# The first batch item in another order: score tile 4 and the second half of q behind score tile 0, fewer zero matmuls, value and score products ahead of hidden tile 1

## The chip, the core and the metric

The kernel runs on one core of one Trainium2 chip. A core has a matrix engine (TensorE, in the profile PE, with its weight loads as PEld), a vector engine (VectorE, DVE), a scalar engine (ScalarE, ACT), a general engine (GpSimd, POOL) and a queue engine (SyncE, SP), each with its own instruction stream. They wait for each other through semaphores. Matrix products land in an accumulator memory that TensorE writes and that VectorE or ScalarE must empty. The metric is device microseconds of one launch, the median of several runs.

## The reference

Four batch items of attention feed a two-branch feed-forward block. What is computed, cut to what matters:

```python
# q, k, v: [4, 8, 768, 64]; sort_net: [4, 8, 8, 8]
P = sort_net
for _ in range(5):                       # Sinkhorn: rows, then columns
    P = exp(P - max(P)); P /= sum(P, -1) + 1e-9; P /= sum(P, -2) + 1e-9
k_sorted = einsum('bhij,bhjcd->bhicd', P, k_blocks)      # 8 blocks of 96 tokens
v_sorted = einsum('bhij,bhjcd->bhicd', P, v_blocks)
attn = softmax(q_block @ k_sorted_block.T / 8)           # block against its own block
x = (attn @ v_sorted_block).transpose(0, 2, 1, 3).reshape(3072, 512)
out = maximum(x @ w1, x @ w2) @ w_out                    # 512 -> 1024 -> 512
```

The kernel uses max(h1, h2) = relu(h1 - h2) + h2: it multiplies x by w1 - w2, takes relu, multiplies by w_out, and adds x times the product w2 @ w_out, which it computes once.

## The kernel before

**Work and names.** Each of the four batch items passes through the same steps. `sort_k` (three calls) and `sort_v` (four calls for one item) mix the blocks of k and v by the Sinkhorn matrix. `q_transposes(b, half)` turns q, in two halves: half 0 has head pairs 0 and 1, half 1 has head pairs 2 and 3. `scores(b, u)` makes score tile u of eight (SC[u] below): u = 4 x ih + hp, block half ih and head pair hp, so tiles 0, 1, 4 and 5 read half 0 of q and tiles 2, 3, 6 and 7 read half 1. Its eight products (L461) land in an accumulator, and ScalarE writes their exponentials into a tile e (L469). `values(b, u)` (VA[u]) multiplies e by v with a column of ones (L488); VectorE takes the reciprocal of the sums (L499) and writes the normalised x (L505). `x_transposes(b, t)` turns two neighbouring value tiles into xT: t = 0 needs value tiles 0 and 1, t = 1 needs 2 and 3, t = 2 needs 4 and 5, t = 3 needs 6 and 7; for item 0 TensorE turns them (L526) and ScalarE copies them out (L108). `moe_h(b, ch, t)` makes hidden tile t of token half ch: eight products (L590) and relu into g. For item 0, hidden tile 0 is made in two parts: the products on head pairs 0 and 2 once xT 0 is there, those on 1 and 3 once xT 1 is there. `w_difference(t)` subtracts a quarter of w2 from w1 (L194): quarters 0 and 1 on GpSimd, 2 and 3 on VectorE; hidden tile t needs quarter t. `w2_transposes(t, eng)` turns half of w2 (L551), and `w_product` multiplies it by w_out (L570). `moe_out` makes output tiles (L617).

**Zero matmuls.** `keep_streaming(ps, n, by, most)` issues products of a tile of zeros into an accumulator, n columns in all, `most` columns at a time; nothing reads them. The kernel begins with 88 of 138 columns (L666), and has 6 of 512 in each of the last two Sinkhorn rounds; the calls with a third number above 0 in the list below have them too. `q_transposes` for item 0 begins each half with one transposition of zeros (L362).

**What sets the order.** Every engine executes its instructions in the order in which the Python program issues them. For item 0 this order is written out by hand, from L665 to L722. Three engines take part in it: TensorE makes the products, VectorE and ScalarE empty the accumulators as the letters "D" and "A" say. There are four accumulators of 4 KB per partition, all of one pool, so a new product has to wait until one of them has been read. After item 0 a planner interleaves hidden and output tiles of one item (the `units`) with the attention steps of the next: after unit n it first issues the list `tail[n]`, then so many steps that they keep pace with the units' cost. `evac` without a letter and `moe_h` take the engine that has less load by the planner's own count. GpSimd issues the loads from HBM; SyncE issues the stores of the output and, from item 1 on, the transposing DMAs.

Of the kernel before, what the change touches and what calls it, by code (L numbers as in the profile page):

```python
# [16 lines left out]
def kernel(  # L17
# [21 lines left out]
    B, H, S, D = q.shape  # L39
# [26 lines left out]
    def ps_f32(name):  # L66
        return psum.tile([128, 1024], FP32, tag="ps", name=name)

    def ps_bf16(name):
        return psum.tile([128, 2048], BF16, tag="ps", name=name)  # L70
# [6 lines left out]
    def keep_streaming(ps, n, by=None, most=512):  # L77

        w0 = fill[:, 0:128] if by is None else late[by]
        while n > 0:  # L80
            w = min(n, most)
            nc.tensor.matmul(ps[:, 0:w], w0, fill[:, 0:w], start=True, stop=True)  # L82
            n -= w
# [265 lines left out]
    def q_transposes(b, half, eng=None):  # L349

        if half == 0:
            qT[b] = qpool.tile([128, HP, R, 128], BF16, tag="qT", name="qT")
        if b > 1:
            hps = slice(half * 2, half * 2 + 2)
            nc.sync.dma_start_transpose(
                out=qT[b][:, hps].rearrange("p h r c -> p (h r) c"),
                in_=q_pair[b][:, hps].rearrange("p h r d -> p (h r d)"),
            )
            return
        ps = ps_bf16("tq_ps")  # L360
        if b == 0:
            nc.tensor.matmul(  # L362
                ps[:, 0:128], fill[:, 0:128], ident, is_transpose=True, start=True, stop=True
            )
        for n in range(2 * R):
            hp, r = half * 2 + n // R, n % R
            c = slice(n * 128, (n + 1) * 128)
            for h2 in range(2):
                nc.tensor.matmul(  # L369
                    ps[h2 * 64 : h2 * 64 + 64, c],  # L370
                    q_raw[b][:, hp + 4 * h2, r * D : (r + 1) * D],
                    ident,
                    is_transpose=True,
                    start=True,
                    stop=True,
                )
        evac(
            qT[b][:, half * 2 : half * 2 + 2].rearrange("p h r c -> p (h r c)"),
            ps[:, 0 : 2 * R * 128],
            2 * R * 128,  # L380
            two_x=True,
            eng=eng,
        )

    def sort_k(b, t, n=0, eng=None):
        kv = k_raw[b].rearrange("p (c d) -> p c d", d=D)
        ps = ps_f32("k_ps")
        keep_streaming(ps, n)

        for c in range(16):  # L390
            for par in range(2):
                m = (c + 8 * par) % 16
                r0 = par * 64
                nc.tensor.matmul(  # L394
                    ps[r0 : r0 + 64, m * 64 : (m + 1) * 64],
                    kv[r0 : r0 + 64, t * 16 + m, :],
                    bd_k[b][r0 : r0 + 64, :],
                    start=True,
                    stop=True,
                )  # L400
        evac(
            kT[b][:, 0 : 32 * BLK]
            .rearrange("p (m ch c) -> p ch m c", ch=2, m=32)[:, :, :, t * 16 : (t + 1) * 16],
            ps.rearrange("p (c ch m) -> p ch m c", ch=2, m=32),
            1024,
            eng=eng,
        )
# [44 lines left out]
    def scores(b, u, n=0):  # L452
        ih, hp = divmod(u, HP)
        ps = ps_f32("s_ps")
        keep_streaming(ps, n)
        for ii in range(4):
            i = ih * 4 + ii
            for h2 in range(2):
                rows = slice(h2 * 64, h2 * 64 + 64)
                rhs = qT[b][rows, hp, :, i * PB : (i + 1) * PB]  # L460
                nc.tensor.matmul(  # L461
                    ps[:, h2 * 512 + ii * 128 : h2 * 512 + ii * 128 + BLK],
                    kT[b][rows, (hp * 8 + i) * BLK : (hp * 8 + i) * BLK + 128],
                    rhs,
                    start=True,
                    stop=True,
                )
        e = e_bufs[(b * 8 + u) % NE]
        nc.scalar.activation(  # L469
            out=e[:, 0 : 8 * BLK].rearrange("p (t c r) -> p t c r", t=8, r=R),  # L470
            in_=ps[0:BLK]
            .rearrange("p (t f) -> p t f", t=8)[:, :, 0:BLK]
            .rearrange("p t (r c) -> p t c r", r=R),
            func=AF.Exp,
            scale=scale,
        )
        load["A"] += 800
        e_tiles[b, u] = e

    def values(b, u, n=0):  # L480
        ih, hp = divmod(u, HP)
        e = e_tiles.pop((b, u))
        m0 = (b % 2) * 64
        ps = ps_f32("o_ps")
        keep_streaming(ps, n)
        for h2 in range(2):
            for ii in range(4):
                nc.tensor.matmul(  # L488
                    ps[:, h2 * 512 + ii * 65 : h2 * 512 + (ii + 1) * 65],
                    e[:, (h2 * 4 + ii) * BLK : (h2 * 4 + ii) * BLK + 128],  # L490
                    v_sb[:, m0 + (hp + 4 * h2) * 8 + ih * 4 + ii, 0:65],
                    start=True,
                    stop=True,
                )
        ov = ps[0:BLK].rearrange("p (t f) -> p t f", t=2)[:, :, 0 : 4 * 65].rearrange(
            "p t (i f) -> p t i f", f=65
        )
        rs = xpool.tile([BLK, 2, 4], FP32, tag="rs", name="rs")
        nc.vector.reciprocal(out=rs, in_=ov[:, :, :, 64])  # L499
        if hp % 2 == 0:  # L500
            x_tiles[b, ih, hp // 2] = xpool.tile(
                [BLK, 2, 4, 2, D], BF16, tag="x", name="x", bufs=4
            )
        x = x_tiles[b, ih, hp // 2][:, :, :, hp % 2, :]
        nc.vector.tensor_tensor(  # L505
            out=x,
            in0=ov[:, :, :, 0:D],
            in1=rs.to_broadcast([BLK, 2, 4, D]),
            op=ALU.mult,
        )  # L510
        load["D"] += 900
# [35 lines left out]
    def w2_transposes(t, eng):  # L547
        ps = ps_bf16("tw_ps")
        for n in range(16):
            fb, dmt = t * 4 + n // 4, n % 4  # L550
            nc.tensor.matmul(  # L551
                ps[:, n * 128 : (n + 1) * 128],
                w2_sb[:, dmt, fb * 128 : (fb + 1) * 128],
                ident,
                is_transpose=True,
                start=True,
                stop=True,
            )
        return lambda: evac(
            w2T[:, t * 4 : t * 4 + 4, :].rearrange("p f d -> p (f d)"),  # L560
            ps,
            2048,
            two_x=True,
            eng=eng,
        )
# [32 lines left out]
    def moe_h(b, ch, t, eng=None, hps=(0, 2, 1, 3), n=0):  # L598
        moe_h_products(b, ch, t, hps, n)
        ps = h_ps[t]  # L600
        g = gpool.tile([128, 2, TCH], BF16, tag="g", name="g")
        src = ps.rearrange("p (t f) -> p t f", t=2)[:, :, 0:TCH]
        if (eng or pick((200 + 2 * TCH) / 1.2, (130 + 2 * TCH) / 0.96)) == "A":
            nc.scalar.activation(out=g, in_=src, func=AF.Relu)  # L604
        else:
            nc.vector.tensor_scalar(
                out=g, in0=src, scalar1=0.0, scalar2=None, op0=ALU.max
            )
        g_tiles[b, ch, t] = g
# [53 lines left out]
        return SC, VA, TR  # L663

    first, second, both = slice(0, 64), slice(64, 128), slice(0, 128)  # L665
    keep_streaming(ps_f32("fill_ps"), 88 * 138, most=138)  # L666
    for it in range(5):
        sinkhorn(it)
        if it < 2:
# [9 lines left out]
    turn_v(first, "D", 80, 96)  # L679

    SC, VA, TR = att(0)
    sort_k(0, 0, 2048, "A")
    sort_k(0, 1, 0, "D")
    sort_k(0, 2, 0, "A")
    sort_v(0, 0, 0, "D")
# [2 lines left out]
    sort_v(0, 2, 0, "A")  # L688
    sort_v(0, 3, 0, "D")
    SC[0]()  # L690
    SC[1]()
    q_transposes(0, 1, "D")
    SC[4]()
    VA[0]()
    scores(0, 2, 1024)
    VA[1]()
    SC[3]()
    values(0, 2, 1024)
    x_transposes(0, 0, "A")
    values(0, 3, 512)  # L700
    SC[5]()
    moe_h_products(0, 0, 0, (0, 2), 512)
    x_transposes(0, 1, "A")
    VA[4]()
    SC[6]()
    moe_h(0, 0, 0, "A", (1, 3))
    SC[7]()
    VA[5]()
    moe_h(0, 0, 1, "A")
    x_transposes(0, 2, "A")  # L710
    VA[6]()
    w_difference(2)
    VA[7]()
    w2_transposes(0, "D")()
    w_difference(3)
    for b in range(1, B):
        selections(b)
    for c, n, m in [(2, 1, 0), (3, 3, 1)]:
# [5 lines left out]
    def turn(rows, c0):  # L724
        turn_v(rows, "D", c0, c0 + 24)
        load["D"] += 850

    def load_rest():
# [1 line left out]
        load_k(2)  # L730

    tail = {
        2: [TR[3], lambda: w2_transposes(1, "A")(), load_rest],
        4: [lambda: turn(second, 0)],
        5: [lambda: block_diagonals([(0, 2), (1, 1), (1, 2), (1, 3)], 2)],
        6: [lambda: turn(second, 24), lambda: turn(second, 48)],
# [6 lines left out]
    for b in range(B):  # L743
# [21 lines left out]
        if b < B - 1:  # L765
            qs = [lambda half=half: q_transposes(b + 1, half) for half in range(2)]
            ks = [lambda t=t, b=b: sort_k(b + 1, t) for t in range(3)]
            SC, VA, TR = att(b + 1)
# [65 lines left out]
```

## Time and profile before

| what | value |
|---|---|
| median of 5 runs | 170.29 us (169.89 to 170.39) |
| the profiled execution | 170.39 us, of which 168.4 us are the span from the first to the last instruction |
| TensorE, matmuls | 162.7 us busy, 97% of the span |
| ScalarE, VectorE, GpSimd | 85.7 us, 75.8 us, 28.6 us |
| 11.7 to 17.5 us (sorting of k and v, half 0 of q) | TensorE busy 5.78 of 5.80 us |
| 17.5 to 24 us (scores, value products) | TensorE busy 6.41 of 6.50 us |
| 24 to 33 us (hidden tiles 0 to 2, the rest of the value products) | TensorE busy 8.31 of 9.00 us |
| 33 to 62 us | TensorE busy 29.00 of 29.00 us |

The page is one profiled execution. A busy time is the union of an engine's instructions; a matmul counts as busy from its start to its modelled end, about 0.2 us for a small one, while the next one starts 15 to 60 ns after it. So an engine that is busy all the time has not necessarily done as much as it could, and zero matmuls count as busy as well. The wait before an instruction is given as idle time, with the instruction that ended it.

### The profile page before, as it was taken

What the parts mean: (1) busy time and instruction counts of PE and PEld (TensorE: products, weight loads), DVE (VectorE), ACT (ScalarE), POOL (GpSimd) and SP (SyncE); (2) the same over time, 40 slices, a digit from 0 to 9 for tenths busy, and PEclk for the clock granted to TensorE, in tenths of its full rate; (3) what the DMA queues carried; (4) which work ended last, traced back from release to release, by engine and by line L of the source; (5) the groups of instructions that cost most, each with busy time, mean ns of one, the idle gap of its engine ahead of it and who ended that gap; (6) DMA issues with size and microseconds to landing.
All of it is one profiled execution on the core that took longest, in us unless ns stands there. A gap on an engine that the chain in (4) does not pass through costs nothing.

```text
span 168.4 us, 4544 instructions
## 1 busy us (share of the span) xinstructions
PE 162.7 (97%) x2018; PEld 97.8 (58%) x2018; DVE 75.8 (45%) x174; ACT 85.7 (51%) x104; POOL 28.6 (17%) x44
## 2 busy tenths in 40 slices
PE   7999999999999999999999999999999999999991
PEld 7949766755765454566654545557545456654451
DVE  4978874948454359437734434205443160000011
ACT  3587878474674353176774504457605406642020
POOL 7866585232302003000000000000000000000000
PEclk9999999999999999999999999999999999999999
DMA  3999999999999994999700344690054255000333
GB/s 46 205 204 198 199 208 206 222 202 204 218 212 206 205 238 81 181 150 234 163 0 4 88 130 141 99 292 5 0 36 139 57 167 171 0 0 0 125 143 110
DMA packets 30243, 23.11 MB, mean 137 GB/s; under 512 B 16720, under 2 KB 25168, under 8 KB 30224
## 3 DMA queue, kind: packets, MB, share of 16 engines
q0 software_dynamic: 10880, 12.59, 44.8%
q1 hardware_dynamic: 19200, 10.17, 25.5%
q8 instruction: 16, 0.26, 0.7%
q10 hardware_dynamic: 144, 0.07, 0.1%
q14 instruction: 3, 0.02, 0.0%
HBM read 25.17 MB, written 6.29 MB: 187 GB/s over the span
## 4 chain that ended last, share of the span: by engine, by line
PE 93%; DVE 2%; ACT 1%; issue 1%
PE out_ps L617 36%; PE h_ps L590 25%; PE fill_ps L82 6%; PE o_ps L488 4%; PE wc_ps L570 4%; PE k_ps L394 4%; PE s_ps L461 4%; PE v_ps L415 2%; PE tq_ps L369 2%; PE v_ps L436 1%; PE tx_ps L526 1%; ACT v_sb L108 1%; PE k_ps L82 1%; DVE q_pair L343 1%; PE tw_ps L551 1%
## 5 line engine op out<-in xcount | busy, mean ns | idle before, releaser
L617 PE MATMUL out_ps<-wo_sb,g 128*128 128x512 bf16 (+2 forms) x200 | 48.5, 371 | 0.3 <-DVE x L505 0.3
L590 PE MATMUL h_ps<-xT,w_sb 128*128 128x384 bf16 x256 | 44.7, 326 | 0.6 <-ACT xT L108 0.4
L590 PEld LDWEIGHTS <-w_sb 128*128 128x128 bf16 x256 | 24.0, 98 | 16.4 <-DVE w_sb L194 0.4
L108 ACT COPY o<-out_ps 128x1024 f32<-128x1024 f32 x11 | 11.1, 1012 | 40.4 <-issue 22.8
L604 ACT ACTIVATE g<-h_ps 128x768 bf16<-128x768 f32 x27 | 21.9, 811 | 16.4 <-PE h_ps L590 16.4
L469 ACT ACTIVATE e<-s_ps 96x768 bf16<-96x768 f32 x32 | 24.3, 805 | 6.1 <-PE s_ps L461 6.1
L617 PEld LDWEIGHTS <-g 128*128 128x128 bf16 x200 | 16.9, 98 | 15.7 <-DVE x L505 0.4
L617 PE MATMUL out_ps<-wc,xT 128*128 128x512 bf16 (+2 forms) x100 | 24.8, 370 | 0.0
L505 DVE TENSOR_TENSOR x<-o_ps,rs 96x512 bf16<-96x512 f32 x32 | 22.0, 687 | 1.1
L499 DVE RECIPROCAL rs<-o_ps 96x8 f32<-96x8 f32 x32 | 6.5, 203 | 33.8 <-PE o_ps L488 33.6
L617 PEld LDWEIGHTS <-xT 128*128 128x128 bf16 x100 | 9.6, 97 | 11.2
L488 PEld LDWEIGHTS <-e 96*128 96x128 bf16 x256 | 11.7, 98 | 6.0 <-ACT e L469 0.2
L488 PE MATMUL o_ps<-v_sb,e 96*128 96x65 bf16 x256 | 12.9, 193 | 0.0
L652 DVE COPY o<-out_ps 128x512 f32<-128x512 f32 (+1 forms) x2 | 1.2, 624 | 25.0 <-PE out_ps L617 25.0
L110 DVE CAST kT<-k_ps 128x1024 bf16<-128x1024 f32 x5 | 6.0, 1222 | 12.3 <-PE k_ps L394 12.3
L110 DVE CAST v_sb<-v_ps 96x1024 bf16<-96x1024 f32 x8 | 9.6, 1215 | 2.5 <-PE v_ps L415 1.7
L108 ACT CAST v_sb<-v_ps 96x1024 bf16<-96x1024 f32 x8 | 8.0, 1005 | 3.3 <-PE v_ps L415 1.9
L136 POOL DMA_DIRECT2D q_raw<-in_q_dram x7 | 6.4, 934 | 19.3 <-DVE rs L499 14.0
L461 PEld LDWEIGHTS <-kT 64*128 64x128 bf16 x256 | 6.1, 94 | 6.1 <-issue 5.2
L82 PEld LDWEIGHTS <-fill 128*128 128x128 bf16 x98 | 8.4, 121 | 1.6 <-DVE fill L73 1.2
L82 PE MATMUL fill_ps<-fill 128*128 128x138 bf16 x88 | 7.8, 272 | 1.2 <-DVE fill L73 1.2
L461 PE MATMUL s_ps<-qT,kT 64*128 64x96 bf16 x256 | 8.8, 204 | 0.1
(77 smaller groups left out, 137.8 us busy)
## 6 DMA issues: line engine op xcount, KB each, us to landing
out_dram<-o SPq DMA_DIRECT2D x11, 512.0 KB, 3.0
k_raw<-in_k_dram POOLq DMA_DIRECT2D x12, 256.0 KB, 12.4
v_raw<-in_v_dram POOLq DMA_DIRECT2D x6, 384.0 KB, 12.8
q_raw<-in_q_dram POOLq DMA_DIRECT2D x3, 768.0 KB, 11.6
w_sb<-in_moe_w_dram POOLq DMA_DIRECT2D x4, 256.0 KB, 9.5
w_sb<-in_moe_w_dram POOLq DMA_DIRECT2D x2, 512.0 KB, 11.3
wo_sb<-in_moe_w_out_dram POOLq DMA_DIRECT2D x2, 512.0 KB, 14.8
v_raw<-in_v_dram POOLq DMA_DIRECT2D x3, 256.0 KB, 4.8
```

The source lines that it names most:

```text
L82: nc.tensor.matmul(ps[:, 0:w], w0, fill[:, 0:w], start=True, stop=True)
L108: nc.scalar.copy(out=out_ap, in_=in_ap)
L110: nc.vector.tensor_copy(out=out_ap, in_=in_ap)
L394: nc.tensor.matmul(ps[r0 : r0 + 64, m * 64 : (m + 1) * 64], kv[r0 : r0 + 64, t * 16 + m, :], bd_k[b][r0 : r0 + 64, :], start=True, stop=True,)
L461: nc.tensor.matmul(ps[:, h2 * 512 + ii * 128 : h2 * 512 + ii * 128 + BLK], kT[b][rows, (hp * 8 + i) * BLK : (hp * 8 + i) * BLK + 128], rhs ...
L469: nc.scalar.activation(out=e[:, 0 : 8 * BLK].rearrange("p (t c r) -> p t c r", t=8, r=R), in_=ps[0:BLK] .rearrange("p (t f) -> p t f", t=8 ...
L488: nc.tensor.matmul(ps[:, h2 * 512 + ii * 65 : h2 * 512 + (ii + 1) * 65], e[:, (h2 * 4 + ii) * BLK : (h2 * 4 + ii) * BLK + 128], v_sb[:, m0 ...
L505: nc.vector.tensor_tensor(out=x, in0=ov[:, :, :, 0:D], in1=rs.to_broadcast([BLK, 2, 4, D]), op=ALU.mult,)
L570: nc.tensor.matmul(ps[:, 0:512], w2T[:, fb, dmt * 128 : (dmt + 1) * 128], wo_sb[:, fb, :], start=(fb == 0), stop=(fb == NFB - 1),)
L590: nc.tensor.matmul(h_ps[t][:, m * 512 : m * 512 + TCH], w1_sb[:, hp, fb * 128 : (fb + 1) * 128], xT[:, b % 2, ch, hp % 2, hp // 2, :], sta ...
L604: nc.scalar.activation(out=g, in_=src, func=AF.Relu)
L617: nc.tensor.matmul(dst, g_tiles[b, ch, m // 2][:, m % 2, off : off + 128] if m < NFB else xT[:, b % 2, ch, hp % 2, hp // 2, off : off + 12 ...
```

## The change

It concerns item 0 alone, and the zeros.

1. The zero stream at the start has 86 products of 142 columns where it had 88 of 138.
2. The first `sort_k` begins with 1024 zero columns (two products) where it had 2048 (four).
3. The zero transposition stays ahead of half 0 of q, and is gone ahead of half 1.
4. Score tile 4 follows score tile 0, then half 1 of q, then score tile 1. Before, the order was 0, 1, half 1, 4.
5. Score tile 2 has no zeros ahead of it (it had two products); value tile 1 has one (it had none), value tile 2 one (it had two), value tile 3 none (it had one).
6. Value tile 4 follows value tile 3, ahead of score tile 5. Before, it stood behind x transposition 1. Score tile 6 and value tile 5 follow x transposition 1; score tile 7 and value tile 6 stand ahead of hidden tile 1. Before, value tile 5 stood ahead of it and value tile 6 behind x transposition 2.
7. VectorE's subtraction of quarter 3 stands ahead of its copy of the first turned half of w2.
8. The second half of w2 is turned, and the next q and k are loaded, after unit 3 where they were after unit 2.

```diff
         ps = ps_bf16("tq_ps")
-        if b == 0:
+        if b == 0 and half == 0:
             nc.tensor.matmul(
...
-    keep_streaming(ps_f32("fill_ps"), 88 * 138, most=138)
+    keep_streaming(ps_f32("fill_ps"), 86 * 142, most=142)
...
-    sort_k(0, 0, 2048, "A")
+    sort_k(0, 0, 1024, "A")
...
     SC[0]()
+    SC[4]()
+    q_transposes(0, 1, "D")
     SC[1]()
-    q_transposes(0, 1, "D")
-    SC[4]()
     VA[0]()
-    scores(0, 2, 1024)
-    VA[1]()
+    SC[2]()
+    values(0, 1, 512)
     SC[3]()
-    values(0, 2, 1024)
+    values(0, 2, 512)
     x_transposes(0, 0, "A")
-    values(0, 3, 512)
+    VA[3]()
+    VA[4]()
     SC[5]()
     moe_h_products(0, 0, 0, (0, 2), 512)
     x_transposes(0, 1, "A")
-    VA[4]()
     SC[6]()
+    VA[5]()
     moe_h(0, 0, 0, "A", (1, 3))
     SC[7]()
-    VA[5]()
+    VA[6]()
     moe_h(0, 0, 1, "A")
     x_transposes(0, 2, "A")
-    VA[6]()
     w_difference(2)
     VA[7]()
-    w2_transposes(0, "D")()
+    w2T_ready = w2_transposes(0, "D")
     w_difference(3)
+    w2T_ready()
...
     tail = {
-        2: [TR[3], lambda: w2_transposes(1, "A")(), load_rest],
+        2: [TR[3]],
+        3: [lambda: w2_transposes(1, "A")(), load_rest],
```

## The prediction

> **What bounds the kernel now.** I read the page first, then the chain of work that ended last, then the timeline of the first item instruction by instruction. The page's chain says that TensorE's own stream sets the time:
>
> ```profile
> PE 93%; DVE 2%; ACT 1%; issue 1%
> ```
>
> So a change pays only where it takes TensorE work out, or a wait of TensorE. TensorE's share of busy time (97%) hides that in the first item part of this work is zeros, and that the stretch from 24 to 33 us has 0.69 us of idle time. First the zero stream, by stretches of a microsecond (TensorE's busy time, and in brackets how many matmuls touch the stretch):
>
> ```profile
> 5.00:6.00 1.00, 1.00 (x12) 1.00 1.09 217
> 6.00:7.00 1.00, 1.00 (x17) 1.00 1.05 209
> 7.00:8.00 1.00, 1.00 (x20) 1.00 1.04 195
> ```
>
> Its products start 115 ns apart until 6.2 us and 60 ns apart after: the clock doubles there, though the column for the granted clock shows 1.00 throughout. Then the timeline (start, length, engine, line, operation, count, idle time before it):
>
> ```profile
> 18.11 0.22 PE L362 MATMUL tq_ps<-ident,fill 128*128 128x128 bf16 x1
> ...
> 19.16 0.96 DVE L110 COPY qT<-tq_ps 128x1536 bf16<-128x1536 bf16 x1 [0.42 <-PE tq_ps L369]
> ...
> 19.58 0.59 PE L82 MATMUL s_ps<-fill 128*128 128x512 bf16 x2
> ...
> 20.17 0.45 PE L461 MATMUL s_ps<-qT,kT 64*128 64x96 bf16 x8
> ...
> 25.44 0.81 PE L590 MATMUL h_ps<-xT,w_sb 128*128 128x384 bf16 x4 [0.37 <-ACT xT L108]
> ...
> 28.22 0.81 ACT L604 ACTIVATE g<-h_ps 128x768 bf16<-128x768 f32 x1 [0.42 <-PE h_ps L590]
> 28.32 0.57 PEld L488 LDWEIGHTS <-e 96*128 96x128 bf16 x16
> 28.36 0.65 PE L488 MATMUL o_ps<-v_sb,e 96*128 96x65 bf16 x16
> ...
> 29.08 1.05 PE L551 MATMUL tw_ps<-ident,w_sb 128*128 128x128 bf16 x16
> ...
> 29.65 0.68 DVE L194 TENSOR_TENSOR w_sb<-w_sb 128x1024 bf16<-128x1024 bf16 x1
> ...
> 30.38 1.47 PE L590 MATMUL h_ps<-xT,w_sb 128*128 128x384 bf16 x8 [0.25 <-DVE w_sb L194]
> ```
>
> To be seen: score tile 2 at 20.17 follows the copy of q's second half (19.16 + 0.96 = 20.12), so its two zeros only fill a wait. The second part of hidden tile 0 (25.44) waits 0.37 us for ScalarE's copy of xT 1. The turning of w2 could follow the last value product (issued by 28.82), but starts at 29.08, when ScalarE has emptied an accumulator (hidden tile 1: 28.22 + 0.81 = 29.03). Hidden tile 2 (30.38) waits for the subtraction of quarter 2 on VectorE (29.65 + 0.68 = 30.33), which stands behind value tile 6.
>
> **What the Trainium skill says.** "TensorE: Matmul & The Clock Gate", Part 1: the array runs at half rate until a window of about 3.4 us has been busy, and falls back after an idle one; a warm matmul costs its columns at 2.4 GHz and about 2.5 ns. The trace agrees in the rates (138 columns: 115 ns and 60 ns). The same page, Part 4 (PE-mode transpose): transpositions don't count as busy for that gate; no run here shows it. No page gives the share of activity from which a window counts as busy.
>
> **The change part by part.** I walk TensorE through the new order. A step starts when the one before it has issued its products (from start to next start: 8 score products 0.27, 8 value products 0.25, 8 x transpositions 0.34, 4 and 8 hidden products 0.65 to 0.75 and 1.30, 16 w2 transpositions 0.91, a zero product 0.22 us), or some 0.04 us after what it waits for.
>
> *Zero stream.* Until 6.235 us it costs the same for any width. Cold, 5.04 us hold 42.6 products of 142 columns (118 ns) where they held 44. The other 43.4 cost 61.7 ns each, 2.68 us, against 44 x 60 ns = 2.64 us. The twelve late zeros follow without a gap, and the first real product (11.56) starts when they are done, not when the Sinkhorn result is there (VectorE, 11.37). So +0.04.
>
> *First sort_k, two zeros fewer* (0.43 us of TensorE): it starts at 12.74 because VectorE's block diagonal is ready at 12.68 to 12.70. Worth 0; TensorE idles there instead.
>
> *Half 1 of q.* The accumulator comes free at 18.06 (ScalarE's v copy) before and after. Without the zero transposition the 24 products start at 18.09 instead of 18.25. Score tile 1: 18.89 (tile 4 was at 19.05), value tile 0: 19.16 (19.32). Exponentials of tile 4 now run on ScalarE before those of tile 1, which are ready at 19.33 + 0.81 = 20.14, and value tile 1 comes later than that. So -0.16.
>
> *Score tile 2 without zeros.* VectorE's copy of half 1 runs from 18.99 to 19.95, tile 2 starts at 20.01 (20.17). The zeros' place becomes a wait of 0.5 us: worth 0 beyond the -0.16.
>
> *To x transposition 0.* Zero 20.28, value tile 1 20.50, score tile 3 20.84, zero 21.12, value tile 2 21.34, done by 21.60. Transposition 0 waits for x 1: products end 20.93, reciprocal and multiply to 21.88, so 21.94 (21.99). Of the 0.16 us, 0.05 remain.
>
> *To hidden tile 0.* Value tiles 3 and 4 from 22.28, score tile 5 22.87, done 23.14. The four accumulators now hold transposition 0, value tiles 3 and 4 and score tile 5, so the hidden tile's zero must wait for ScalarE's copy of xT 0 (22.48 + 0.80), starts at 23.34 and keeps the first hidden products until 23.57. Before, the zero ran ahead of that copy, and they started at 23.40. So +0.17.
>
> *To hidden tile 1.* Transposition 1 24.22, score tile 6 24.56, value tile 5 24.83, done 25.08. ScalarE copies xT 1 from 24.76 to 25.56: the second part starts at 25.62 (25.44), +0.17, after a wait of 0.54 us. Score tile 7 26.37, value tile 6 26.64, hidden tile 1 26.88 (26.72). The order is as long as before here, but has one value tile more behind it.
>
> *Behind hidden tile 1.* x transposition 2 28.19, then one value tile (7) where there were two: 28.53 to 28.78, -0.25. The accumulator for w2 is now that of value tile 6, read by 28.0, no longer that of hidden tile 1: no wait, -0.2; w2 starts at 28.79 (29.08). Value tile 6 done earlier puts the subtraction of quarter 2 at 27.93 to 28.61 on VectorE, so hidden tile 2 follows the transpositions at 29.70 (30.38): -0.39. Transposition 3 31.00; quarter 3 is subtracted by 30.50, so hidden tile 3 comes at 31.35, the rest of w2 at 32.66, hidden tile 4 at 33.57. Before, it started 1.30 us after 32.96, at 34.26. Sum: +0.17 - 0.25 - 0.2 - 0.39 = -0.67 or -0.68.
>
> *Moves without a price.* The second w2 copy now runs on ScalarE behind the relu of hidden tile 3, until about 35.6; its reader, the product at L570, comes at 39.2. Quarter 3 ahead of the first w2 copy delays that copy to 31.63, and it has the same reader. The loads that move behind unit 3 keep their place in GpSimd's queue, which holds no TensorE work and waits for earlier loads to land.
>
> *Later.* TensorE is busy 29.00 of 29.00 us from 33 to 62, so it carries the gain on. At 66.42 it waits 0.25 us for VectorE, whose chain starts from value products of TensorE at 62.64, so it moves along.
>
> Total: -0.68 + 0.04 = -0.64, say -0.6 us, in the profiled execution 170.39 to 169.8. This execution is the slowest of the five; from the median of 170.29 I come to **169.7**. The bound for a difference that can be told is 0.2%, 0.34 us.
>
> **Rivals.** *Most of the gain stays out* (18%): the waits behind hidden tile 1 return. If w2 has to wait for the relu of hidden tile 1 as before (28.39 + 0.81 = 29.20), hidden tile 2 starts at 30.15 instead of 30.38; with +0.04 that is -0.2 us: 170.1. For it: it takes only another rotation of accumulators than I count, or more loss in the waits ahead of hidden tile 1. Against: the order of allocation. A gain lost in the VectorE stage at 66 us ends at 170.3, in the same case.
>
> *The clock falls back* (12%), slower than before. New idle stretches are 0.44 us at 12.3, 0.5 at 19.5, 0.25 at 21.7, 0.2 at 23.2 and 0.54 at 25.1, where the zeros stood or the order waits. None is near 3.4 us, but by the columns issued the emptiest 3.4 us (from 18.6) fall from about 65% of the array's time to some 52%, partly transpositions. One window at half rate doubles the work in it: between 1.0 us (1.8 us of work, less idle time that absorbs it) in the thin stretch and 3.4 us in the dense hidden tiles; with -0.6 that is 170.7 to 173.1, at the middle 171.6. It decides as soon as more than 0.6 us of work is doubled.
>
> *The change undoes nothing* (in the second case): its zeros were only cover. That holds for the zeros, but not for the two waits behind hidden tile 1.
>
> **How the numbers follow.** My forecast has 70%: 169.3 (another 0.4 us, about the waits that I leave at 20 and 25 us) to 170.0. The second case fills 169.95 to 170.6, the third 170.7 up. From 169.3 to 170.4 I count 68 of the 70 and some 13 of the 18 points. The bounds of the unknown: the start of the clock's doubling can differ from run to run, at 60 ns per 115 ns of delay (the five runs spread over 0.5 us), which moves the median by some 0.1 us either way. Faster 0.70, same 0.17, slower 0.13.
>
> **What would show it.** Right: sort_k at about 12.78; score tile 2 at 20.0 after VectorE's copy; the zero ahead of hidden tile 0 behind ScalarE's copy; a wait of about 0.5 us for xT 1; no wait ahead of w2 and of hidden tile 2; hidden tile 4 near 33.6. Wrong: matmuls of 384 columns more than 200 ns apart after 12 us (the clock), or hidden tile 2 at 30 us or later.

## The result, and the profile after

| | before | after |
|---|---|---|
| median | 170.41 us (169.87 to 171.72, 80 runs) | 171.37 us (170.53 to 174.01, 43 runs) |
| ratio to before, 95% interval | | 1.0048 [1.0035, 1.0061] |
| profiled execution, span | 170.39 us, 168.4 us | 170.76 us, 168.9 us |

The changed kernel is slower by 0.5%, where I had forecast a gain. About a third of its executions (13 of 44, the profiled one counted) lie a further 2 to 3 us up; none of those was profiled, the ratio leaves out ten of them, and they are not explained here. The profiled execution took 170.76 us, 0.6 us below the median.

The page's chain of after still names TensorE, with 2% of the span in which it waited for nothing that the profile shows (1% before):

```profile
PE 91%; DVE 3%; ACT 2%; issue 2%
```

The timeline of after, over the first item (start, length, engine, line, operation, count, idle time before it):

```profile
12.62 1.70 PE L394 MATMUL k_ps<-bd,k_raw 64*64 64x64 bf16 x96 [0.42 <-DVE bd L321]
...
17.98 0.86 PE L369 MATMUL tq_ps<-ident,q_raw 128*64 128x128 bf16 x24
...
18.88 0.96 DVE L110 COPY qT<-tq_ps 128x1536 bf16<-128x1536 bf16 x1 [0.27 <-PE tq_ps L369]
...
19.89 0.34 PE L461 MATMUL s_ps<-qT,kT 64*128 64x96 bf16 x8 [0.43 <-DVE qT L110]
...
20.46 0.39 PE L82 MATMUL o_ps<-fill 128*128 128x512 bf16 x1 [0.23 <-PE s_ps L461]
...
22.67 0.80 ACT L108 COPY xT<-tx_ps 128x768 bf16<-128x768 bf16 x1 [0.45 <-PE tx_ps L526]
...
23.52 0.38 PE L82 MATMUL h_ps<-fill 128*128 128x512 bf16 x1
...
25.77 0.81 PE L590 MATMUL h_ps<-xT,w_sb 128*128 128x384 bf16 x4 [0.26 <-ACT xT L108]
...
28.09 0.68 DVE L194 TENSOR_TENSOR w_sb<-w_sb 128x1024 bf16<-128x1024 bf16 x1
...
28.94 1.06 PE L551 MATMUL tw_ps<-ident,w_sb 128*128 128x128 bf16 x16
...
29.83 1.46 PE L590 MATMUL h_ps<-xT,w_sb 128*128 128x384 bf16 x8
...
33.67 0.65 PE L590 MATMUL h_ps<-xT,w_sb 128*128 128x384 bf16 x3
```

The order does what was worked out for it: no wait ahead of the turning of w2 (28.94) and none ahead of hidden tile 2 (29.83), and hidden tile 4 starts at 33.67 where it started at 34.26. Up to here after is 0.59 us ahead, 0.12 us of it because its first `sort_k` began that much earlier (12.62 against 12.74). Then it loses more than that in one place. The waits of TensorE in after (who waited, for whom; us in total, times, longest):

```profile
PE fill_ps L82 <- DVE fill L73: 1.2, 1, 1.2
PE v_ps L415 <- issue: 0.9, 1, 0.9
PE s_ps L461 <- DVE qT L110: 0.4, 1, 0.4
...
```

The second line was not there before. The timeline of after around it, of all engines:

```profile
45.31 0.71 PE L415 MATMUL v_ps<-bd,v_dc 64*128 64x64 bf16 x19
45.43 0.47 PEld L415 LDWEIGHTS <-v_dc 64*128 64x128 bf16 x14
...
46.91 0.09 PEld L415 LDWEIGHTS <-v_dc 64*128 64x128 bf16 x1 [1.01 <-issue]
46.91 0.20 PE L415 MATMUL v_ps<-bd,v_dc 64*128 64x64 bf16 x1 [0.89 <-issue]
47.05 0.47 PE L369 MATMUL tq_ps<-ident,q_raw 128*64 128x128 bf16 x10
```

TensorE stands in the middle of a step: 47 of the 48 products of one `sort_v` of item 1 are issued, the 48th comes 1.07 us after the 47th (start to start). It reads the same v and block diagonal as the products around it, and writes the same accumulator. Its weight load, which no product holds up, stands as long. So I take it that the instruction is missing, not its data. The sum closes: 0.59 us gained, 1.07 lost, +0.48; the span grew from 168.4 to 168.9 us.

**Where the instruction is.** The page lists a queue of the kind "instruction": 16 packets of 16 KB before, 15 after (the trace of after has a sixteenth at 169.12 us, 0.2 us behind the last instruction). TensorE issues weight loads and matmuls in pairs, one load and the product that uses it (2,018 of each before, 2,010 after), and at 128 pairs to a packet 2,018 pairs need 15.8 packets; so I take this to be TensorE's own program, in blocks of 256 instructions. The Trainium skill, "Runtime: NRT & Kernel Launch", section "Instruction fetch mechanics", says the same of the block: an engine's program comes in blocks of 16 KiB, 256 instructions, which its sequencer fetches itself over a DMA queue while it executes the block before. It adds that crossing a block boundary costs "one DMA tail-bump, mostly hidden". Here it was not hidden. The DMA view, cut to two stretches; first before (16 engines; the first line is their busy share in 40 slices, the last names the packet that started in the stretch):

```profile
DMA  4989904889994889998884998844998484998098
...
q8 instruction: 1, 0.02, 5.8%
```

This is the stretch from 42.9 to 43.9 us of before. The same packet in after stands in the stretch from 44.5 to 45.5 us; from 38 to 44.4 us no packet of that queue started:

```profile
DMA  9994894999998888899098899499499999490949
...
q8 instruction: 1, 0.02, 5.9%
```

The trace's packet records give it to 10 ns. This is the fifth block that is fetched while the kernel runs. I call it block 5; its first instruction belongs to about pair 733 of TensorE's stream, and TensorE enters the block ahead of it at about pair 605.

| | before | after |
|---|---|---|
| TensorE enters the block ahead | 41.86 us | 41.38 us |
| packet of block 5 starts, has landed | 42.95, 43.88 us | 44.51, 45.46 us |
| TensorE comes to the first instruction of block 5 | 46.23 us, 2.35 after the landing | 45.87 us, 0.41 after the landing |
| and issues it | at once | 46.91 us, 1.45 after the landing |

The change made TensorE come earlier, and the block later. At both times the DMA engines are nearly full with the loads of k and v.

The zero stream in after, in stretches of a microsecond as shown of before (busy time, matmuls in brackets, granted clock, DMA share, GB/s):

```profile
5.00:6.00 1.00, 1.00 (x14) 1.00 1.04 201
6.00:7.00 1.00, 1.00 (x20) 1.00 1.07 207
```

The rate doubled at 5.66 us in this execution, at 6.22 in that of before. The Trainium skill, "TensorE: Matmul & The Clock Gate", Part 1, says that this moment differs from run to run, by 500 ns to either side. These two traces differ by 0.56 us, which fits; but the twelve profiles of this document have it between 4.36 and 6.78 us, which is more than that. With it the first `sort_k` moves, from 12.45 to 13.03 us, so times of steps from two profiles can differ by some tenths of a microsecond by chance.

### The profile page after: what moved, and what is told of

Same layout as the page of the kernel before. It is cut to its first block, busy times and chain, and to the rows that moved or that the text cites. A ratio compares the mean times of both kernels' runs of the same rounds, so it can differ in the third digit from the quotient of the medians.

```text
span 168.9 us, 4530 instructions
## 1 busy us (share of the span) xinstructions
PE 161.3 (96%) x2010; PEld 97.3 (58%) x2010; DVE 75.8 (45%) x174; ACT 86.0 (51%) x104; POOL 28.6 (17%) x44
## 3 DMA queue, kind: packets, MB, share of 16 engines
q0 software_dynamic: 10880, 12.59, 44.5%
## 4 chain that ended last, share of the span: by engine, by line
PE 91%; DVE 3%; ACT 2%; issue 2%
PE out_ps L617 36%; PE h_ps L590 25%; PE fill_ps L82 6%; PE wc_ps L570 4%; PE k_ps L394 4%; PE o_ps L488 4%; PE s_ps L461 3%; PE v_ps L415 2%; PE tq_ps L369 2%; PE v_ps L436 1%; PE tw_ps L551 1%; ACT xT L108 1%; PE tx_ps L526 1%; DVE x L505 1%; ACT v_sb L108 1%
## 5 line engine op out<-in xcount | busy, mean ns | idle before, releaser
L82 PEld LDWEIGHTS <-fill 128*128 128x128 bf16 x91 | 7.8, 120 | 1.8 <-DVE fill L73 1.2
L82 PE MATMUL fill_ps<-fill 128*128 128x142 bf16 x86 | 7.6, 269 | 1.2 <-DVE fill L73 1.2
```

## The experiments

**The theory (F, where an expectation uses a letter):** the 8 pairs that the change takes out of TensorE's stream, all of zeros, move every later block boundary by 8 pairs against the work. Block 5 is now asked for behind the products of the first `w_product` (L570, 0.23 us a pair, 1.83 us for 8) where it was asked for ahead of most of them, and comes too late. **The rival (O):** the new order itself sets the wait at 46 us, by the place where its steps and transfers now fall, and the number of instructions has nothing to do with it. The zero stream can tell them apart. Its number of products is free as long as its columns, and so its time, stay about the same (86 x 142 = 12,212 columns).

**The changed order with as many instructions as before.** 94 pairs in the zero stream give 2,018.

```diff
-    keep_streaming(ps_f32("fill_ps"), 86 * 142, most=142)
+    keep_streaming(ps_f32("fill_ps"), 94 * 130, most=130)
```

> The changed kernel with its zero stream cut as 94 products of 130 columns (12,220 columns against 12,212), so that TensorE's stream is as long in instructions as that of the kernel before. Theory F (TensorE's own program, fetched in blocks of 16 KB, came too late: 16 instructions fewer put the point that calls for the fifth block behind the 1.83 us of the first w_product instead of ahead of it): no idle time inside the third v product of item 1 at 46 us, the fetch starts near 42.5 us instead of 44.5, and the time is 0.4 to 0.6 us below before, some 169.9. Theory O (the wait comes of the new order itself, TensorE meeting the loads 0.6 us earlier): the wait of some 0.9 us stays, and the time is 0.4 to 0.6% above before.

Measured: 169.99 us (before in the same comparison: 170.51), ratio 0.9966 [0.9949, 0.9982]. The packet of block 5 starts at 42.50 us, and the wait at 46 us is gone. The order is the changed one; so it is the count, not the order. The wait at 20.5 us is still there, now ahead of score tile 2. TensorE's timeline of this kernel:

```profile
20.52 0.34 PE L461 MATMUL s_ps<-qT,kT 64*128 64x96 bf16 x8 [0.68 <-ACT e L469]
```

The profile names ScalarE, which had long been done. The products start 0.87 us after the instruction ahead of them, part of that the usual wait for the copy of q (which ended at 20.21), and 1.44 us after block 2 landed.

**The old order with 16 instructions fewer.** The reverse: nothing but the zero stream is changed in before.

```diff
-    keep_streaming(ps_f32("fill_ps"), 88 * 138, most=138)
+    keep_streaming(ps_f32("fill_ps"), 80 * 152, most=152)
```

> The kernel before with nothing changed but its zero stream: 80 products of 152 columns (12,160 against 12,144), which takes 16 instructions out of TensorE's stream and leaves the order alone. Theory F: the same idle stretch of about 1 us appears in the third v product of item 1, and the time rises by 0.6 to 1.1 us, to about 171.3. Theory O: nothing happens, 170.4, at most 0.1 us from 16 columns more.

Measured: 172.92 us, ratio 1.0171 [1.0140, 1.0201]. The direction is as expected, the size is not: three blocks are late now. TensorE's timeline:

```profile
15.58 0.26 PE L415 MATMUL v_ps<-bd,v_dc 64*128 64x64 bf16 x3 [0.47 <-issue]
...
21.78 0.39 PE L488 MATMUL o_ps<-v_sb,e 96*128 96x65 bf16 x7 [0.78 <-issue]
...
48.58 0.64 PE L369 MATMUL tq_ps<-ident,q_raw 128*64 128x128 bf16 x16 [0.73 <-ACT v_sb L108]
```

These are pairs 223, 351 and 734 (the first is 0), each 1.30 to 1.60 us after a landing. The first two are 128 apart, the third is 383 further, one short of three times 128; a few instructions that are neither weight load nor product would make that difference, but the trace doesn't show them. The idle times sum to 1.98 us, and the profiled span grew by 2.0 (170.4 against 168.4). The median grew by 2.4; the profiled execution has the shortest span of the six (170.4 to 171.6).

**A dose, half of it each time.** The changed order with 2 pairs and with 4 pairs more.

```diff
-    keep_streaming(ps_f32("fill_ps"), 86 * 142, most=142)
+    keep_streaming(ps_f32("fill_ps"), 88 * 139, most=139)
```

> The changed kernel with 88 products of 139 columns: 4 instructions more. Theory F: the call for the block moves 4 instructions of 0.114 us into the first w_product, so the wait of about 1.04 us (from start to start) shrinks by some 0.4 us to about 0.6; the time falls by 0.4 us. Theory O: no change beyond the 20 columns (0.01 us).

```diff
-    keep_streaming(ps_f32("fill_ps"), 86 * 142, most=142)
+    keep_streaming(ps_f32("fill_ps"), 90 * 136, most=136)
```

> The changed kernel with 90 products of 136 columns: 8 instructions more. Theory F: the call comes 8 instructions, 0.9 us, earlier: 0.1 to 0.3 us of the wait are left, and the time is 0.7 to 0.9 us below the changed kernel's. Theory O: no change.

Measured: with 2 pairs 169.90 us, 0.9962 [0.9948, 0.9975]; with 4 pairs 169.69 us, 0.9961 [0.9946, 0.9976]. Two pairs were expected to take 0.4 us off the wait at 46 us, and took all of it: the block landed at 44.59, and TensorE came to it 1.45 us later, just late enough. A wait at 20.55 us (0.58 us start to start) stayed. With 4 pairs, measured in four executions only, the list of TensorE's waits names no late block any more; it has these six:

```profile
PE fill_ps L82 <- DVE fill L73: 1.2, 1, 1.2
PE s_ps L461 <- DVE qT L110: 0.4, 1, 0.4
PE k_ps L394 <- DVE bd L321: 0.4, 1, 0.4
PE h_ps L590 <- ACT xT L108: 0.3, 1, 0.3
PE out_ps L617 <- DVE x L505: 0.3, 1, 0.3
PE tx_ps L526 <- DVE x L505: 0.2, 1, 0.2
```

Both kernels came out faster than expected: the ratio to before fell by 0.9%, which is 1.5 us, where 0.4 us and 0.7 to 0.9 us were forecast.

The list leaves out short waits, because a small matmul counts as busy for about 0.2 us. Block 2 begins at pair 351, in score tile 2 or next to it, and it is late in all twelve profiles: the pair stands 1.30 to 1.60 us behind the landing in each. With 90 products it falls into the tile:

```profile
19.77 0.53 PE L461 MATMUL s_ps<-qT,kT 64*128 64x96 bf16 x8 [0.43 <-DVE qT L110]
```

These eight products and what follows them are 0.46 us apart, start to start, where 0.27 is usual. In before it is 0.38 us: pair 351 starts at 20.27, 0.10 us behind pair 350 and 1.60 us behind the landing at 18.67. The line of score tile 2 that the prediction shows (20.17) has the mark of it, 0.45 us where such a tile usually takes 0.34. Part of the lateness is hidden there, since the tile waits for the copy of q until 20.12 anyway.

The kernels for which every matmul is in the trace show the dose for block 5; the third column is how long after TensorE had entered the block ahead the packet of block 5 started:

| kernel | pairs in the stream | packet starts after | wait for block 5, start to start |
|---|---|---|---|
| after | 2,010 | 3.13 us | 1.07 us |
| old order, 16 instructions fewer | 2,010 | 3.08 | 0.92 us |
| changed order, 88 products | 2,012 | 2.11 | 0 |
| changed order, 90 products | 2,014 | 1.61 | 0 |
| changed order, 94 products | 2,018 | 0.91 | 0 |
| before | 2,018 | 1.09 | 0 |

Eight pairs change the start by some 2.0 to 2.2 us in both orders, and the eight products of `w_product` that stand there take 1.83 us.

**Without the load that fills the DMA engines.** The loads of k and v for items 2 and 3 are left out, so what these two items compute is not what the reference asks for; TensorE's work and its instructions are those of after.

```diff
     def load_k(b):
+        if b > 1:
+            k_raw[b] = k_raw[b - 2]
+            return
...
     def load_v(b, c0=0, pieces=2):
+        if b > 1:
+            return
```

> The changed kernel as it is, 86 products of 142 columns, but the loads of k and v for items 2 and 3 are left out: items 2 and 3 are computed from the k and v of items 0 and 1, so the output of these two items is another. All instructions of TensorE stay. Theory F with its second half (the fetch is slow because the DMA engines are full of loads, 3.5 us from the call to the start of the packet where it takes 1.0 to 1.2 us at 90 us and later): the fetch near 41 us starts within 1.5 us of its call, there is no wait in the third v product of item 1, and the time falls by about 1 us against the changed kernel, to some 0.3% below before. If the fetch starts as late as before, the loads are not what holds it, and the wait stays.

Measured: 170.13 us, 0.9962 [0.9941, 0.9983]. The DMA view from 42.6 to 44 us, where after is nearly full:

```profile
DMA  2911111121111211000000000000000000000000
...
q8 instruction: 1, 0.02, 5.6%
```

The packet starts at 42.66 us, about 0.7 us after TensorE entered the block ahead, with 2,010 pairs as in after, and there is no wait at 46 us. So two things have to meet: a call that comes late in the stream, and DMA engines so full that the packet starts only 3.13 us after the boundary. At 20 us, where the loads are still there, the wait stays (0.61 us).

**The changed order without its two cover zeros.** If the prediction's walk is right, the zeros ahead of value tile 1 and of hidden tile 0 lie on the path, and without them hidden tile 0 starts when ScalarE has copied xT 0. The number of pairs stays at 2,014.

```diff
-    keep_streaming(ps_f32("fill_ps"), 86 * 142, most=142)
+    keep_streaming(ps_f32("fill_ps"), 92 * 133, most=133)
...
-    values(0, 1, 512)
+    VA[1]()
...
-    moe_h_products(0, 0, 0, (0, 2), 512)
+    moe_h_products(0, 0, 0, (0, 2))
```

> The changed kernel with 92 products of 133 columns (as many instructions in all as with 90 of 136) and without the zero products ahead of value tile 1 and of hidden tile 0. By my steps, value tile 1 comes 0.22 us earlier and pulls x transposition 0 and ScalarE's copy of xT 0 with it, and the first hidden products start with that copy instead of 0.22 us after it: 0.44 us below the kernel with 90 of 136, 1.0 us (0.6%) below before, some 169.4. Rivals: the two places gain nothing because another wait takes over (0.4% below before), or the clock falls back without these zeros (above before).

Measured: 169.17 us in six executions, 0.9914 [0.9882, 0.9947]. This beats both kernels. Its timeline:

```profile
22.23 0.80 ACT L108 COPY xT<-tx_ps 128x768 bf16<-128x768 bf16 x1 [0.38 <-PE tx_ps L526]
...
23.08 0.81 PE L590 MATMUL h_ps<-xT,w_sb 128*128 128x384 bf16 x4
...
33.02 1.46 PE L590 MATMUL h_ps<-xT,w_sb 128*128 128x384 bf16 x8
```

Hidden tile 0 (23.08) follows the copy (22.23 + 0.80 = 23.03), and hidden tile 4 comes at 33.02, 0.42 us ahead of the kernel with 90 products.

**Which half of the order brings the gain.** The first half of the change (up to value tile 2, and the zeros) with the old second half; and the old first half with the new order from value tile 3 on. Both have a number of pairs at which block 5 comes in time (2,014 and 2,017). The diffs are against after, the second one cut.

```diff
-    keep_streaming(ps_f32("fill_ps"), 86 * 142, most=142)
+    keep_streaming(ps_f32("fill_ps"), 90 * 136, most=136)
...
     VA[3]()
-    VA[4]()
     SC[5]()
...
+    VA[4]()
     SC[6]()
-    VA[5]()
...
     SC[7]()
-    VA[6]()
+    VA[5]()
...
     x_transposes(0, 2, "A")
+    VA[6]()
     w_difference(2)
     VA[7]()
-    w2T_ready = w2_transposes(0, "D")
+    w2_transposes(0, "D")()
     w_difference(3)
-    w2T_ready()
...
-        2: [TR[3]],
-        3: [lambda: w2_transposes(1, "A")(), load_rest],
+        2: [TR[3], lambda: w2_transposes(1, "A")(), load_rest],
```

> Only the first half of the change, with 90 products of 136 columns: fewer zeros, score tile 4 ahead, up to x transposition 0; from value tile 3 on the order and the list behind unit 2 of the kernel before (value tile 3 without zeros). By my steps 0.05 us are left at x transposition 0 and the waits behind hidden tile 1 stay: within 0.1 us of before. If the zeros removed were worth their own time, it would be 0.8 us below.

```diff
-    keep_streaming(ps_f32("fill_ps"), 86 * 142, most=142)
+    keep_streaming(ps_f32("fill_ps"), 88 * 138, most=138)
...
-    sort_k(0, 0, 1024, "A")
+    sort_k(0, 0, 2048, "A")
...
-    SC[4]()
+    SC[1]()
     q_transposes(0, 1, "D")
-    SC[1]()
+    SC[4]()
     VA[0]()
-    SC[2]()
-    values(0, 1, 512)
+    scores(0, 2, 1024)
+    VA[1]()
...
```

> Only the second half of the change: the kernel before with its zero stream, all zeros and the score order up to x transposition 0, and from value tile 3 on the new order (value tile 3 without zeros) with the new lists behind units 2 and 3. By my steps this is the whole gain: 0.6 us (0.37%) below before, hidden tile 4 at 33.6. Rival: the new order needs the earlier start of its first half, and gains less than 0.3 us.

Measured: the first half alone 170.60 us, 0.9989 [0.9966, 1.0013]; the second alone 169.82 us, 0.9959 [0.9941, 0.9978], as much as the whole (0.9961), though block 2 is late in it too, at 20.4 us. With the first half alone, score tile 2 comes 0.15 us sooner behind the first `sort_k` than in before (7.28 against 7.42 us); by hidden tile 4 that is gone (21.46 against 21.41 us, without what block 2 takes in each), as the prediction had it. So far as intervals of some 0.2% can tell, the whole gain is in the second half: value tiles and the subtraction ahead of what waits for them.

**The old order with 4 instructions more, and after once more.**

```diff
-    keep_streaming(ps_f32("fill_ps"), 88 * 138, most=138)
+    keep_streaming(ps_f32("fill_ps"), 90 * 135, most=135)
```

> The kernel before with 90 products of 135 columns (12,150 against 12,144): 4 instructions more, nothing else. Theory F: the calls for the blocks move 4 instructions forward, where the kernel before has no such wait to lose, so within 0.2% of before, 170.4. If more instructions were a gain in themselves, as they are in the changed kernel, it would be 0.3 to 0.6 us below.

> The changed kernel as it is, once more. Theory F: waits without a named cause again only at the places where a new block of 128 weight loads and matmuls begins (about product pairs 351 and 733), each 1.3 to 1.6 us after the landing of a fetch, and the time 0.3 to 0.7% above before. If the wait of the first profile was a chance event, it is missing here and the time is 0.4% below before.

Measured: 170.84 us, 1.0017 [0.9996, 1.0038], and for after 171.50 us, 1.0051 [1.0030, 1.0072]. The old order doesn't gain from more pairs. It is within the 0.2% expected, but not without a wait: block 2 is late at 20.5 us, 0.8 us behind the pair ahead of it. A second profile of after has both waits again, and the same instruction stands at 47.27 us, 1.50 us after its block landed:

```profile
47.27 0.20 PE L415 MATMUL v_ps<-bd,v_dc 64*128 64x64 bf16 x1 [0.93 <-issue]
```

## Why the prediction was wrong

Predicted was 169.7 us, from a sum of -0.64 us, faster at 0.70; measured is 1.0048 times before.

| step | predicted | after | changed order, 90 products |
|---|---|---|---|
| score tile 2, behind the copy of half 1 | 20.01 | 19.89 | 19.77 |
| zero of hidden tile 0, behind the copy of xT 0 | 23.34 | 23.52 | 23.29 |
| second part of hidden tile 0, behind the copy of xT 1 | 25.62 | 25.77 | 25.54 |
| turning of w2, no wait | 28.79 | 28.94 | 28.70 |
| hidden tile 2, no wait | 29.70 | 29.83 | 29.60 |
| hidden tile 4 | 33.57 | 33.67 | 33.44 |

**Right: the walk through item 0.** Every step stands within 0.2 us of its predicted time in after, but part of that is luck: the first `sort_k` was put at 12.78 and began at 12.62 in after and at 12.49 with 90 products, as the clock doubled earlier in these executions. Counted from step to step (the walk itself starts from the 12.74 of before, and adds the 0.04 us of the zero stream at its end):

| from, to | predicted | after | changed order, 90 products |
|---|---|---|---|
| first `sort_k`, score tile 2 | 7.27 | 7.28 | 7.28 |
| score tile 2, zero of value tile 1 | 0.27 | 0.57 | 0.46 |
| zero of value tile 1, hidden tile 4 | 13.29 | 13.20 | 13.20 |

The walk is right to 0.1 us everywhere but in the middle row, and there block 2 is late. The changed order with 90 products, in which block 5 is in time, is 0.39% faster. That this is 0.66 us of 170.5, beside the 0.64 predicted, is closer than its interval of 0.4 to 0.9 us can tell. The two zeros of `sort_k` and those ahead of score tile 2 were only cover, as said: a wait of 0.42 and 0.43 us took their place. The second case, in which the waits behind hidden tile 1 return, did not come. Nor did the clock fall back: the hidden products stay 162 ns apart.

**Smaller terms.** The zero stream was put at +0.04 us; in this execution the moment of the doubling decided, and the first real product came 0.12 us earlier (11.44 against 11.56), now behind the Sinkhorn result on VectorE and no longer behind the zeros. The zero ahead of value tile 1 was put at 20.28 and came at 20.46, though score tile 2 had started 0.12 us ahead of its forecast; that is block 2, late by 0.30 us in after.

**Wrong: the step "Later. TensorE is busy 29.00 of 29.00 us from 33 to 62, so it carries the gain on."** Being busy without a gap was a statement on the stream of before, and I took it for one on the steps. It held because block 5 came in time, 2.35 us ahead of its use, of which 1.3 to 1.6 us are needed. With that went a second one: I costed the instructions that were removed by their columns and their time alone. That they also stand in a row with all later ones, and that taking 16 out moves where the row is cut, was in no term of the sum. Its size: 1.07 us at 46.9 us. Block 2 adds to it at 20.5 us, with 0.30 us where before lost 0.11. The measured 171.37 us lies in the range of the rival "the clock falls back", but its reason did not occur: that is luck.

The profile of before did hold two signs. One is the list of queues: 16 packets of 16 KB on a queue of the kind "instruction"; I did not ask when these started, nor which instruction stood at their boundaries. The other is score tile 2, whose line I had before me: it took 0.11 us too long, at a boundary. What I could have said from them is that one block is already just late, and that 8 pairs fewer put the boundary of another between steps of very unlike length, beside full DMA queues. That block 5 would be late by 1.07 us could not be told from before alone.

**What stays open.** Where in the stream a block is asked for is my inference, not in a record: the starts in the table fit a call some 16 to 20 pairs ahead of the boundary of the block before. Why a block serves only 1.3 to 1.6 us after it has landed is not shown either. Each kernel but after has one profile, so how late its blocks are in other executions is not known. The medians moved by more than the profiles: from after to 88 products the ratio to before fell by 0.9% (1.5 us), the profiled span by 0.8 us. Some of that lies outside the span. In every execution of the kernels with 2,012 pairs or more whose span is on record, the time is 1.8 to 2.0 us longer than the span; with 2,010 pairs it is 2.1 to 3.7 us longer in 28 of 82 executions. In three of the four profiles with 2,010 pairs the last packet of the instruction queue starts behind the last instruction (169.12 us in after), and in those of the other kernels 4.6 to 7.2 us ahead of it. Whether the one is the cause of the other was not tested.

## What to carry to other kernels

When an edit adds or removes instructions of an engine with a long unrolled stream, ask for the packets of the instruction queue: when each starts and lands, and how long after it the engine comes to the block's first instruction. Here a wait without a releaser in the middle of a step, weight load and product alike, at about the same number of instructions modulo 256, was a block that came late; where the profile named an engine, that engine had long been done. A short lateness is in no list of waits, only in a step that takes longer than its like. Shift the stream by a few instructions before you judge the edit, here with zeros of the same total width. An edit's worth is then the difference between two kernels whose blocks come equally in time, which before and the kernel with 90 products nearly are (0.11 and 0.19 us late): the change was worth -0.66 us, the late block 5 +1.07.

## What the runs showed of the hardware

- TensorE's program comes in blocks of 256 instructions (16 KB), and the next one is fetched some time around when the one before is entered: in after the first six packets start 1.6 to 3.6 us behind that, later ones up to 2.1 us ahead of it. In dense stretches of small matmuls 128 pairs take 4.5 to 5.1 us (from 14.94 to 20.03, and from 41.38 to 45.84 in after), which is then about all the time that the fetch has.
- The packets of the late blocks took 0.9 to 1.2 us from start to landing, and the first instruction of such a block ran 1.30 us after the landing at the earliest, 1.60 at the latest. A block that TensorE came to 2.35 us after the landing cost nothing.
- How long the packet waits to start depends on the loads: 3.13 us after the boundary with DMA engines near full, about 0.7 us with the loads gone, at the same place in the stream. The skill's "mostly hidden" holds nearly in before and with 90 products (0.11 and 0.19 us in sight), and not in after.
- Sixteen instructions in a stream of 4,036, with the total of zero columns nearly the same, cost 2.4 us where they were taken out of before (170.51 to 172.92), and brought the ratio from 1.0048 to 0.9966 where they were put back into after.
- The doubling of TensorE's rate came between 4.36 and 6.78 us in the twelve profiles, with the zero stream begun at 1.19 us in each.
